# Sixteen last sums on GpSimd, eleven transposed copies on VectorE and a new order in an attention and highway kernel

## The chip, the cores and the metric

The kernel runs on one core of a Trainium2 chip. The metric is the device time of one execution in microseconds (us), median over runs. The engines are named as in the profile: PE (TensorE, matmuls), PEld (its weight loads), DVE (VectorE), ACT (ScalarE), POOL (GpSimd) and SP (SyncE, which here only issues DMAs).

## The reference

Sliding-window attention with four sink keys, then a highway layer. Batch 4, 8 heads, 768 positions, head size 64; the highway layer has 3072 tokens of 512.

```python
scores = scale * (q @ k.T)
keep = is_sink | ((rel >= 0) & (rel < 128))      # rel = query position - key position
a = exp(where(keep, scores, -1e9) - max);  a = a / (sum(a) + 1e-9)
x = (a @ v), heads side by side                  # (3072, 512)
H = maximum(x @ w_h, 0)
T = 1 / (1 + exp(-(x @ w_t + b_t)))
out = T * H + (1 - T) * x                        # float32
```

## The kernel before

The 3072 tokens are 24 tiles of 128; six tiles make a batch. A tile n goes through these steps, each a small function of the kernel:

- Loads: lq, lk, lv. Tiles 0 and 1 of q and k come in float32 through SP (q) and ACT (k), and DVE casts them (cvq, cvk). All others, v and the weights (lw_t, lw_h) are issued by POOL and cast on the way; each q or k tile of POOL goes into one of eight buffers. For batches 1 to 3, v comes in two halves (lv0, lv1).
- T (L258) transposes q and k on PE into PSUM, cT (L272) copies them to SBUF on ACT. pks (L278) puts a batch's four sink keys aside with small POOL copies, and issues the next batch's sink values.
- S0, S1 (L304) are the scores of four heads each, for this tile's keys and those of the tile before; E0, E1 (L320) their exponentials on ACT into float16; M0, M1 (L329) multiply them with a 0/1 mask on DVE, both inputs in SBUF. sk and es do the sink keys for two tiles.
- BA (L344) starts the tile's PSUM sum with the sink part, AV (L353) adds the weighted values and, in column 64 of each head, the sums of the weights. rec (L375) is their reciprocal on DVE, x (L380) the division on DVE out of PSUM, into xh.
- X (L387) transposes xh on PE, cX copies it to SBUF as xT: on ACT, or on DVE where the step is named cXd (L397).
- Tt (L407) and H (L422) multiply xT with the two weight matrices, four matmuls of 512 columns each. u (L417) is a tanh on ACT. On DVE: d (L430) is max(H, 0) - x, with H in PSUM; g (L436) turns the tanh into the sigmoid, SBUF to SBUF; ee (L442) is g * d, both in SBUF; od (L447) is the last sum xh + ee, both float16 in SBUF, into float32, and the SP queue stores it.

Constants: K1 to K5 (L210 to L244), pm and pb (L194 to L208, selects on POOL that make masks), lbt (L216, two loads of the bias on SP). K2 sets the bias rows, with two casts of one row of 512 on DVE (L227). A few matmuls on a zero tile (_FILL, L20) keep PE busy early.

The order is written out by hand: _STEPS (L21 to L55) is one list of steps, and each engine and each DMA queue takes its instructions in the order of that list. An instruction that waits holds up all that is behind it on its engine; a DMA issued by POOL stands in one line with POOL's computing. Buffers: four each for u, dd, gt and ee and for the output tile, seven each for xh and xT, one PSUM buffer for AV's and X's results.

Of the kernel before, what the change touches and what calls it, by code (L numbers as in the profile page):

```python
# [11 lines left out]
ALU = mybir.AluOpType  # L12
# [6 lines left out]

_FILL = {'T:0': 4, 'S1:0': 3, 'T:1': 1, 'S1:1': 3, 'S0:1': 2, 'S1:2': 1, 'T:3': 3}  # L20
_STEPS = """  # L21
    lk:0 lq:2 lsv:0 K4:0 pm:0 K1:0 cvk:0 lk:1 lbt:0 lq:0 cvq:0 T:0 cT:0 K3:0 S1:0 E1:0 S0:0 E0:0
    cvk:1 lq:1 cvq:1 T:1 K2:0 lq:3 lv:0 M1:0 cT:1 S1:1 E1:1 S0:1 M0:0 AV:0 lk:2 lk:3 rec:0 x:0 T:3
    E0:1 lv:1 T:2 M1:1 X:0 cT:2 cXd:0 M0:1 S0:2 AV:1 rec:1 x:1 cT:3 S1:3 lw_t:0 lk:4 pb:0 K5:0 pks:0
    E0:2 sv:6 E1:3 M1:3 M0:2 lq:4 S1:2 E1:2 sk:2 es:2 X:1 cX:1 Tt:0 u:0 T:4 cT:4 S0:3 lv:2 M1:2 E0:3
    lw_h:0 BA:2 AV:2 rec:2 x:2 M0:3 Tt:1 u:1 lq:5 g:1 lk:5 g:0 lv:3 X:2 cX:2 S1:4 H:0 d:0 E1:4 M1:4
    H:1 lq:7 T:5 S0:4 d:1 lk:7 ee:1 cT:5 E0:4 BA:3 AV:3 rec:3 lq:6 Tt:2 u:2 sk:4 es:4 x:3 od:1 X:3
    cX:3 S1:5 g:2 ee:0 M0:4 lv:4 E1:5 H:2 S0:5 d:2 E0:5 BA:4 AV:4 od:0 rec:4 lk:6 T:6 lv:5 ee:2 x:4
    cT:6 od:2 lv0:6 Tt:3 M0:5 u:3 X:4 lk:8 cX:4 T:7 cT:7 M1:5 S0:6 H:3 BA:5 AV:5 d:3 g:3 ee:3 lq:8
    E0:6 S1:6 E1:6 rec:5 S0:7 x:5 Tt:4 X:5 od:3 M1:6 E0:7 M0:7 u:4 g:4 T:8 S1:7 lv1:6 cX:5 E1:7 M0:6  # L30
    H:4 Tt:5 lk:9 d:4 lq:9 AV:6 M1:7 cT:8 u:5 ee:4 lk:10 S1:8 E1:8 rec:6 lq:10 x:6 pks:6 H:5 X:6
    od:4 d:5 S0:8 g:5 ee:5 T:9 cX:6 AV:7 rec:7 x:7 lk:11 Tt:6 E0:8 X:7 od:5 cT:9 S1:9 cXd:7 u:6 sk:8
    M0:8 lq:11 lk:13 g:6 E1:9 lk:12 es:8 lq:12 H:6 lq:13 T:10 cT:10 M1:8 d:6 ee:6 S0:9 E0:9 BA:8
    AV:8 rec:8 Tt:7 u:7 T:11 lk:14 cT:11 x:8 X:8 S1:10 od:6 cXd:8 H:7 M0:9 BA:9 E1:10 M1:9 S0:10 d:7
    AV:9 E0:10 rec:9 x:9 g:7 ee:7 M0:10 Tt:8 lq:14 u:8 T:12 X:9 od:7 g:8 cT:12 M1:10 lv0:12 cX:9
    sk:10 es:10 H:8 d:8 S1:11 E1:11 S0:11 E0:11 sv:12 BA:10 AV:10 rec:10 x:10 Tt:9 T:13 ee:8 u:9
    S0:12 E0:12 M1:11 X:10 lv1:12 M0:11 H:9 M0:12 S1:12 cX:10 BA:11 pks:12 lk:15 od:8 AV:11 rec:11
    cT:13 g:9 E1:12 T:14 cT:14 Tt:10 x:11 X:11 cX:11 d:9 ee:9 M1:12 S1:13 S0:13 H:10 od:9 u:10 g:10
    AV:12 rec:12 x:12 E0:13 Tt:11 lq:15 T:15 d:10 M0:13 E1:13 M1:13 lk:18 ee:10 u:11 g:11 X:12 S1:14
    H:11 d:11 cX:12 E1:14 cT:15 AV:13 od:10 S0:14 E0:14 Tt:12 sk:14 u:12 es:14 ee:11 S1:15 E1:15  # L40
    rec:13 lq:17 S0:15 x:13 X:13 od:11 lk:17 lk:16 M0:14 cX:13 M1:14 H:12 d:12 lq:20 T:17 g:12 BA:14
    AV:14 rec:14 x:14 E0:15 lq:16 T:16 M0:15 cT:17 lq:18 ee:12 Tt:13 X:14 lv0:18 M1:15 cT:16 H:13
    cX:14 S1:16 S0:16 u:13 d:13 od:12 E1:16 E0:16 lq:19 BA:15 lv1:18 g:13 AV:15 sk:16 rec:15 ee:13
    S0:17 es:16 E0:17 Tt:14 u:14 x:15 od:13 lk:19 lk:20 S1:17 M0:16 X:15 cX:15 E1:17 H:14 T:18 BA:16
    M1:16 M0:17 AV:16 d:14 Tt:15 cT:18 S0:18 T:19 pks:18 rec:16 g:14 u:15 x:16 X:16 cX:16 E0:18
    ee:14 od:14 H:15 M1:17 BA:17 M0:18 S1:18 g:15 lq:21 d:15 AV:17 rec:17 x:17 Tt:16 lk:21 cT:19
    S1:19 ee:15 E1:18 M1:18 T:20 X:17 cXd:17 u:16 g:16 H:16 od:15 AV:18 cT:20 E1:19 lq:22 rec:18
    x:18 S0:19 d:16 E0:19 M0:19 M1:19 Tt:17 u:17 S1:20 X:18 T:21 cX:18 H:17 cT:21 ee:16 lk:22 AV:19
    d:17 T:22 rec:19 E1:20 x:19 od:16 cT:22 g:17 sk:20 es:20 sv:18 S0:20 ee:17 M1:20 E0:20 M0:20
    X:19 Tt:18 u:18 lq:23 cX:19 od:17 H:18 d:18 S0:21 E0:21 S1:21 E1:21 BA:20 AV:20 rec:20 g:18  # L50
    lk:23 Tt:19 T:23 S1:22 u:19 x:20 M0:21 X:20 cX:20 ee:18 M1:21 cT:23 od:18 g:19 H:19 d:19 BA:21
    AV:21 E1:22 rec:21 S0:22 E0:22 Tt:20 ee:19 x:21 u:20 od:19 M0:22 M1:22 sk:22 S1:23 X:21 cX:21
    S0:23 H:20 es:22 BA:22 AV:22 g:20 d:20 rec:22 x:22 ee:20 E1:23 E0:23 M0:23 Tt:21 u:21 X:22 cX:22
    H:21 M1:23 BA:23 AV:23 d:21 g:21 rec:23 x:23 od:20 Tt:22 u:22 ee:21 g:22 od:21 X:23 cX:23 H:22
    d:22 ee:22 od:22 Tt:23 u:23 g:23 H:23 d:23 ee:23 od:23  # L55
"""


# [1 line left out]
def kernel(  # L60
# [13 lines left out]
    nc = tc.nc  # L74
    P = 128

    B, H, S, D = q.shape
# [44 lines left out]
    bt32 = const.tile([P, DM], FP32, tag="bt32")  # L122
    bt16 = const.tile([P, DM], FP16, tag="bt16")
# [70 lines left out]
    def pm():  # L194
        nc.gpsimd.affine_select(
            out=mask[:, 1, :], in_=mask[:, 1, :], compare_op=ALU.is_ge, fill=0.0,
            base=0, pattern=[[1, P]], channel_multiplier=-1)
        nc.gpsimd.affine_select(
            out=mask[:, 0, :], in_=mask[:, 0, :], compare_op=ALU.is_ge, fill=0.0,
            base=-1, pattern=[[-1, P]], channel_multiplier=1)  # L200

    def pb():
        nc.gpsimd.affine_select(
            out=bm, in_=bm, compare_op=ALU.is_ge, fill=0.0,
            base=0, pattern=[[-NSINK, H]], channel_multiplier=1)
        nc.gpsimd.affine_select(
            out=bm, in_=bm, compare_op=ALU.is_ge, fill=0.0,
            base=NSINK - 1, pattern=[[NSINK, H]], channel_multiplier=-1)  # L208

    def K1():  # L210
        nc.vector.tensor_copy(out=mask0, in_=mask[:, 1, :])
        nc.vector.memset(mask0[0:NSINK, :], 1.0)
        nc.vector.tensor_copy(out=mask1, in_=mask)
        nc.vector.memset(mask1[0:NSINK, 0, :], 1.0)

    def load_bt():  # L216
        nc.sync.dma_start(out=bt32[0:1], in_=moe_b_t.unsqueeze(0))
        nc.sync.dma_start(out=bt32[64:65], in_=moe_b_t.unsqueeze(0))

    def K2():  # L220
        nc.vector.memset(bt16, 0.0)
        nc.vector.memset(ones_row, 0.0)
        nc.vector.memset(ones1, 0.0)
        nc.vector.memset(ones1[0:1, :], 1.0)
        for r in (0, 64):
            nc.vector.memset(ones_row[r:r + 1, :], 1.0)
            nc.vector.tensor_copy(out=bt16[r:r + 1, :], in_=bt32[r:r + 1, :])  # L227

    def K3():
        for i in range(2):  # L230
            nc.vector.memset(ks_bd[i], 0.0)

    def K4():
        for vb in v_bat:
            nc.vector.memset(vb[:, 0:VBW].rearrange("p (m e) -> p m e", e=65)[:, :, D:D + 1], 1.0)
            nc.vector.memset(vb[:, VBW:VBW + 8], 0.0)
        for i in range(2):
            nc.vector.memset(vs_bd[i], 0.0)
            nc.vector.memset(es_t[i], 0.0)
# [10 lines left out]
    def warm_up(n):  # L250
        w = m_ps.tile([P, DM], FP32, tag="m", name="wps")
        for _ in range(n):
            nc.tensor.matmul(w, lhsT=warm[:, 0:P], rhs=warm, start=True, stop=True)

    qkT, tp_of, s_of, e_of, av_of, rec_of, g_of = {}, {}, {}, {}, {}, {}, {}
    xtp_of, xh_of, xT_of, t_of, u_of, h_of, dd_of, ee_of, sk_of = {}, {}, {}, {}, {}, {}, {}, {}, {}

# [116 lines left out]

    def rec(n):  # L375
        r = r_pool.tile([P, H], FP32, tag="rec", name="rec")
        nc.vector.reciprocal(out=r.unsqueeze(2), in_=av_of[n][:, :, 64:65])
        rec_of[n] = r

    def x(n):  # L380
# [63 lines left out]
        nc.vector.tensor_tensor(out=e, in0=g_of.pop(n), in1=dd_of.pop(n), op=ALU.mult)  # L444
        ee_of[n] = e

    def o(n):  # L447
        otok = o_pool.tile([P, DM], FP32, tag="otok", name="otok")
        nc.vector.tensor_tensor(out=otok, in0=xh_of.pop(n), in1=ee_of.pop(n), op=ALU.add)  # L449
        nc.sync.dma_start(out=out[n * P:(n + 1) * P, :], in_=otok)  # L450

    run = {
# [3 lines left out]
        "lsv": load_sink_v, "cvq": lambda n: convert("q", n), "cvk": lambda n: convert("k", n),  # L456
        "pm": lambda n: pm(), "pb": lambda n: pb(), "K1": lambda n: K1(), "K2": lambda n: K2(), "lbt": lambda n: load_bt(),
        "K3": lambda n: K3(), "K4": lambda n: K4(), "K5": lambda n: K5(),
        "T": T, "cT": cT, "pks": pks, "sv": lambda n: sink_v(n // NSC, nc.vector), "sk": sk, "es": es,
        "S0": lambda n: scores(n, 0), "S1": lambda n: scores(n, 1),  # L460
        "E0": lambda n: expo(n, 0), "E1": lambda n: expo(n, 1),
        "M0": lambda n: masked(n, 0), "M1": lambda n: masked(n, 1),
        "BA": BA, "AV": AV, "rec": rec, "x": x, "X": X, "cX": cX, "Tt": Tt, "u": u, "H": Hh,
        "cXd": lambda n: cX(n, nc.vector),
        "d": d, "g": g, "ee": ee, "od": o,
    }

    with tc.manual_schedule(engines={ENG.PE, ENG.DVE, ENG.Activation, ENG.SP, ENG.Pool}):
        first()
        for step in _STEPS.split():  # L470
            name, n = step.split(":")
# [36 lines left out]
```

## Time and profile before

| What | Value |
|---|---|
| Runs, us | 115.22, 115.41, 116.79 (median 115.41) |
| The profiled execution, us | 116.29 |
| Its span, first to last instruction, us | 114.6 |
| Mean granted PE clock over the span | 0.986 |
| Busy us: PE, DVE, ACT, POOL | 102.0, 102.2, 91.1, 60.8 |
| Instructions: PE, DVE, ACT, POOL | 1617, 236, 125, 79 |
| HBM read and written, MB | 21.01 and 6.29 |
| q and k loads through POOL | 44 of 128 KB, about 7 us from issue to landing |
| Chain that ended last, by engine | DVE 31%, DMA 24%, PE 19%, POOL 15%, ACT 5% |

In the profile a group is one line of the kernel on one engine: its name is output<-inputs, then the shapes, the count, the busy us of all and the mean ns of one, and the engine's idle time just before them with what ended it. POOL's busy time includes issuing its DMAs. A stretch of the timeline has its start, its length and its work; equal instructions behind one another are merged. The table of stretches has, for each, PE, PEld, DVE, ACT and POOL busy in us with the number of instructions, then the granted clock, the DMA share and GB/s. A row of waits has the engine and line, what it waited for, and us in total, times and the longest. The chain is followed back from the last instruction, at each step to what released it.

### The profile page before, as it was taken

How to read it: one execution, taken by the hardware profiler on the slowest of the kernel's cores; microseconds unless marked ns; L12 is line 12 of the kernel's file. 1: busy time of each engine (PE TensorE's matmuls, PEld its weight loads, DVE VectorE, ACT ScalarE, POOL GpSimd, SP SyncE). 2: the span in 40 equal slices, each digit the busy share in tenths (PEclk: the TensorE clock that was granted, in tenths of full speed). 3: DMA queues.
4: the chain of work that ended last, by engine and by line, in shares of the span. 5: the costliest groups of instructions: out<-in, count | busy, mean ns of one | idle time of the engine just before them, and what ended most of it. 6: DMA issues, size and time to landing. Idle time of an engine off the chain costs nothing.

```text
span 114.6 us, 3853 instructions
## 1 busy us (share of the span) xinstructions
PE 102.0 (89%) x1617; PEld 56.4 (49%) x1617; DVE 102.2 (89%) x236; ACT 91.1 (80%) x125; POOL 60.8 (53%) x79
## 2 busy tenths in 40 slices
PE   5956949999999899999999999999998999999910
PEld 2313535555555455556455655646554655644400
DVE  4649569699999999999999999999997999999990
ACT  3137699979999898989989999998898999982500
POOL 5999999796976199704999980003960000000000
PEclk9999999999999999999999999999999999999995
DMA  2999999999999999999999999991899222220332
GB/s 63 244 161 154 198 162 194 156 157 155 156 191 225 181 207 211 215 156 196 166 129 196 194 168 200 212 220 54 112 134 191 36 91 92 96 93 0 123 152 92
DMA packets 79540, 17.56 MB, mean 153 GB/s; under 512 B 75426, under 2 KB 76450, under 8 KB 79524
## 3 DMA queue, kind: packets, MB, share of 16 engines
q0 software_dynamic: 71904, 9.98, 132.0%
q1 hardware_dynamic: 5540, 6.82, 18.4%
q10 hardware_dynamic: 2080, 0.52, 2.0%
q8 instruction: 12, 0.20, 0.7%
q14 instruction: 4, 0.03, 0.1%
HBM read 21.01 MB, written 6.29 MB: 238 GB/s over the span
## 4 chain that ended last, share of the span: by engine, by line
DVE 31%; DMA 24%; PE 19%; POOL 15%; ACT 5%; issue 3%; POOLq 0%; ACTq 0%
DMA ksd<-in_k_dram 14%; DMA vb<-in_v_dram 10%; DVE e L335 8%; PE hps L426 6%; DVE otok L449 6%; DVE xh L382 5%; DVE dd L432 5%; POOL qsd L150 4%; PE av L368 3%; POOL ksd L150 3%; PE tps L414 3%; POOL v_all L146 3%; PE sps L316 3%; DVE gt L438 2%; DVE ee L444 2%
## 5 line engine op out<-in xcount | busy, mean ns | idle before, releaser
L324 ACT ACTIVATE e<-sps 128x1024 f16<-128x1024 f32 (+1 forms) x48 | 44.8, 961 | 2.2 <-PE sps L316 1.9
L274 ACT COPY qk<-tp 128x1024 f16<-128x1024 f16 x24 | 24.3, 1021 | 7.3 <-PE tp L268 7.3
L335 DVE TENSOR_TENSOR e<-e,mask 128x1024 f16<-128x1024 f16 (+1 forms) x48 | 29.2, 638 | 0.2
L426 PE MATMUL hps<-wh_sb,xT 128*128 128x512 f16 x96 | 24.7, 381 | 0.0
L414 PE MATMUL tps<-wt_sb,xT 128*128 128x512 f16 x96 | 24.7, 379 | 0.0
L150 POOL DMA_DIRECT2D ksd<-in_k_dram x22 | 19.9, 910 | 4.5 <-PE av L368 3.1
L150 POOL DMA_DIRECT2D qsd<-in_q_dram x22 | 20.1, 921 | 0.2
L419 ACT ACTIVATE u<-tps 128x512 f16<-128x512 f32 x24 | 14.5, 606 | 5.6 <-PE tps L414 5.4
L316 PE MATMUL sps<-qk 64*128 64x128 f16 x352 | 16.8, 217 | 1.7 <-ACT qk L274 1.7
L382 DVE TENSOR_TENSOR xh<-av,rec 128x512 f16<-128x512 f32 x24 | 16.5, 689 | 0.6
L432 DVE SCALAR_TENSOR_TENSOR dd<-hps,xh 128x512 f16<-128x512 f32 x24 | 16.4, 681 | 0.7 <-PE hps L426 0.7
L449 DVE TENSOR_TENSOR otok<-xh,ee 128x512 f32<-128x512 f16 x24 | 16.4, 683 | 0.1
L368 PEld LDWEIGHTS <-e 128*128 128x128 f16 x352 | 12.8, 97 | 5.5 <-DVE e L335 2.3
L316 PEld LDWEIGHTS <-qk 64*128 64x128 f16 x352 | 10.7, 94 | 8.6 <-issue 6.5
L404 ACT COPY xT<-xtp 128x512 f16<-128x512 f16 x20 | 11.8, 588 | 1.0 <-PE xtp L393 0.7
L368 PE MATMUL av<-vb,e 128*128 128x66 f16 x264 | 11.6, 194 | 0.6 <-DMA vb<-in_v_dram 0.4
L414 PEld LDWEIGHTS <-xT 128*128 128x128 f16 x96 | 8.2, 97 | 7.3
L426 PEld LDWEIGHTS <-xT 128*128 128x128 f16 x96 | 7.7, 98 | 8.0 <-issue 0.3
L285 POOL COPY ks<-qk 64x16 f16<-64x16 f16 x8 | 2.8, 349 | 16.2 <-ACT qk L274 16.0
L444 DVE TENSOR_TENSOR ee<-gt,dd 128x512 f16<-128x512 f16 x24 | 10.0, 417 | 0.3
L156 POOL DMA_DIRECT2D vb<-in_v_dram x6 | 8.7, 1449 | 1.2 <-DMA ksd<-in_k_dram 1.0
L438 DVE TENSOR_SCALAR gt<-u 128x512 f16<-128x512 f16 x24 | 8.6, 363 | 0.0
(66 smaller groups left out, 110.3 us busy)
## 6 DMA issues: line engine op xcount, KB each, us to landing
out_dram<-otok SPq DMA_DIRECT2D x24, 256.0 KB, 5.1
qsd<-in_q_dram POOLq DMA_DIRECT2D x22, 128.0 KB, 7.3
ksd<-in_k_dram POOLq DMA_DIRECT2D x22, 128.0 KB, 7.0
vb<-in_v_dram POOLq DMA_DIRECT2D x6, 384.0 KB, 10.8
v_all<-in_v_dram POOLq DMA_DIRECT2D x6, 128.0 KB, 7.0
kf<-in_k_dram ACTq DMA_DIRECT2D x2, 256.0 KB, 3.9
qf<-in_q_dram SPq DMA_DIRECT2D x2, 256.0 KB, 5.8
wt_sb<-in_moe_w_t_dram POOLq DMA_DIRECT2D x1, 512.0 KB, 6.9
```

The source lines that it names most:

```text
L150: nc.gpsimd.dma_start(out=sd, in_=dram(x, n))
L274: nc.scalar.copy(out=qk.rearrange("p j (a t) -> p a j t", a=2), in_=tp_of.pop(n)[:, :, 0:DM].rearrange("p a (j t) -> p a j t", t=64))
L316: nc.tensor.matmul(sps[:, hh, o:o + P], lhsT=kk[rows, hp, :], rhs=qT[rows, hp, :], start=True, stop=True)
L324: nc.scalar.activation(out=e.rearrange("p a b c d -> p a (b c d)"), in_=sps[:, :, 0:2 * np_ * P], func=AF.Exp, bias=_EXP_BIAS, scale=SCALE)
L335: nc.vector.tensor_tensor(out=ev, in0=ev, in1=m.unsqueeze(1).to_broadcast([P, 4, np_ * P]), op=ALU.mult)
L368: nc.tensor.matmul(av[:, g, 2 * hl + hh, 0:_AVN], lhsT=e[:, hh, hl, pc, :], rhs=v_cols(m, h), start=fresh, stop=False, skip_group_check=True)
L382: nc.vector.tensor_tensor(out=xh.rearrange("p (h d) -> p h d", d=D), in0=av_of.pop(n)[:, :, 0:D], in1=rec_of.pop(n).unsqueeze(2).to_broadc ...
L414: nc.tensor.matmul(t_of[n], lhsT=xT[:, kc, :], rhs=wt_sb[:, kc, :], start=False, stop=(kc == NOC - 1))
L419: nc.scalar.activation(out=uu, in_=t_of.pop(n), func=AF.Tanh, scale=0.5)
L426: nc.tensor.matmul(hps, lhsT=xT[:, kc, :], rhs=wh_sb[:, kc, :], start=(kc == 0), stop=(kc == NOC - 1))
L432: nc.vector.scalar_tensor_tensor(out=dd, in0=h_of.pop(n), scalar=0.0, in1=xh_of[n], op0=ALU.max, op1=ALU.subtract)
L449: nc.vector.tensor_tensor(out=otok, in0=xh_of.pop(n), in1=ee_of.pop(n), op=ALU.add)
```

## The change

It does five things.

- The last sum has two forms: `od:n` on DVE as before (tiles 0, 1, 2, 4, 6, 9, 15, 23) and `o:n` on POOL (the sixteen others). The POOL form gets a further dependency: it waits for the latest rec that stands ahead of it in the list.
- The copy of x's transpose is on DVE for tiles 0, 3, 4, 8, 10, 13, 14, 15, 16, 19 and 20 (before: 0, 7, 8, 17).
- The two casts of the bias go from K2 on DVE to a step K6 on ACT.
- The memsets of the sink tiles go from K4 to a step K7 that comes later.
- The list has another order throughout. _FILL is as before.

The code:

```diff
@@ -224,7 +224,10 @@
         nc.vector.memset(ones1[0:1, :], 1.0)
         for r in (0, 64):
             nc.vector.memset(ones_row[r:r + 1, :], 1.0)
-            nc.vector.tensor_copy(out=bt16[r:r + 1, :], in_=bt32[r:r + 1, :])
+
+    def K6():
+        for r in (0, 64):
+            nc.scalar.copy(out=bt16[r:r + 1, :], in_=bt32[r:r + 1, :])
 
     def K3():
         for i in range(2):
@@ -234,6 +237,8 @@
         for vb in v_bat:
             nc.vector.memset(vb[:, 0:VBW].rearrange("p (m e) -> p m e", e=65)[:, :, D:D + 1], 1.0)
             nc.vector.memset(vb[:, VBW:VBW + 8], 0.0)
+
+    def K7():
         for i in range(2):
             nc.vector.memset(vs_bd[i], 0.0)
             nc.vector.memset(es_t[i], 0.0)
@@ -252,6 +257,8 @@
         for _ in range(n):
             nc.tensor.matmul(w, lhsT=warm[:, 0:P], rhs=warm, start=True, stop=True)
 
+    last = {}
+    SYNC = mybir.DependencyInfo(mybir.DependencyClass.Sync, mybir.DependencyReason.DATA)
     qkT, tp_of, s_of, e_of, av_of, rec_of, g_of = {}, {}, {}, {}, {}, {}, {}
     xtp_of, xh_of, xT_of, t_of, u_of, h_of, dd_of, ee_of, sk_of = {}, {}, {}, {}, {}, {}, {}, {}, {}
 
@@ -374,7 +381,7 @@
 
     def rec(n):
         r = r_pool.tile([P, H], FP32, tag="rec", name="rec")
-        nc.vector.reciprocal(out=r.unsqueeze(2), in_=av_of[n][:, :, 64:65])
+        last["rec"] = nc.vector.reciprocal(out=r.unsqueeze(2), in_=av_of[n][:, :, 64:65])
         rec_of[n] = r
 
     def x(n):
@@ -444,9 +451,12 @@
         nc.vector.tensor_tensor(out=e, in0=g_of.pop(n), in1=dd_of.pop(n), op=ALU.mult)
         ee_of[n] = e
 
-    def o(n):
+    def o(n, eng):
         otok = o_pool.tile([P, DM], FP32, tag="otok", name="otok")
-        nc.vector.tensor_tensor(out=otok, in0=xh_of.pop(n), in1=ee_of.pop(n), op=ALU.add)
+        add = eng.tensor_tensor(out=otok, in0=xh_of.pop(n), in1=ee_of.pop(n), op=ALU.add)
+        if eng is nc.gpsimd:
+            tc.add_manual_dep(add.ins, last["rec"].ins.name, SYNC,
+                              reason="beside the PSUM reads that follow the reciprocal")
         nc.sync.dma_start(out=out[n * P:(n + 1) * P, :], in_=otok)
 
     run = {
@@ -456,13 +466,14 @@
         "lsv": load_sink_v, "cvq": lambda n: convert("q", n), "cvk": lambda n: convert("k", n),
         "pm": lambda n: pm(), "pb": lambda n: pb(), "K1": lambda n: K1(), "K2": lambda n: K2(), "lbt": lambda n: load_bt(),
         "K3": lambda n: K3(), "K4": lambda n: K4(), "K5": lambda n: K5(),
+        "K6": lambda n: K6(), "K7": lambda n: K7(),
         "T": T, "cT": cT, "pks": pks, "sv": lambda n: sink_v(n // NSC, nc.vector), "sk": sk, "es": es,
         "S0": lambda n: scores(n, 0), "S1": lambda n: scores(n, 1),
         "E0": lambda n: expo(n, 0), "E1": lambda n: expo(n, 1),
         "M0": lambda n: masked(n, 0), "M1": lambda n: masked(n, 1),
         "BA": BA, "AV": AV, "rec": rec, "x": x, "X": X, "cX": cX, "Tt": Tt, "u": u, "H": Hh,
         "cXd": lambda n: cX(n, nc.vector),
-        "d": d, "g": g, "ee": ee, "od": o,
+        "d": d, "g": g, "ee": ee, "o": lambda n: o(n, nc.gpsimd), "od": lambda n: o(n, nc.vector),
     }
 
     with tc.manual_schedule(engines={ENG.PE, ENG.DVE, ENG.Activation, ENG.SP, ENG.Pool}):
```

The new list:

```diff
+    lq:0 lk:0 lq:1 lk:1 lbt:0 lq:3 K4:0 K2:0 lk:2 cvq:0 cvk:0 lv:0 T:0 cT:0 lq:2 pm:0 S1:0 E1:0 K3:0
+    lv:1 lsv:0 cvq:1 lk:3 lw_t:0 pks:0 S0:0 lw_h:0 lk:4 E0:0 K1:0 lq:4 pb:0 cvk:1 K7:0 lv:2 T:1 M0:0
+    cT:1 lk:6 S1:1 E1:1 lk:5 S0:1 M1:0 AV:0 rec:0 x:0 T:2 X:0 cXd:0 E0:1 T:3 K6:0 M1:1 cT:2 S1:2
+    M0:1 cT:3 E1:2 K5:0 AV:1 rec:1 x:1 S1:3 Tt:0 sv:6 lq:5 E1:3 u:0 X:1 S0:2 cX:1 M1:3 E0:2 M1:2
+    lv:3 S0:3 lq:6 sk:2 es:2 lv0:6 lv:4 H:0 d:0 lk:7 BA:2 E0:3 T:4 cT:4 lq:7 M0:2 Tt:1 AV:2 u:1 S1:4
+    lv:5 H:1 M0:3 E1:4 g:0 ee:0 rec:2 x:2 od:0 X:2 cX:2 S0:4 E0:4 d:1 T:5 cT:5 g:1 BA:3 Tt:2 u:2
+    M1:4 ee:1 AV:3 S1:5 E1:5 H:2 lq:8 lk:8 M0:4 T:6 cT:6 rec:3 x:3 X:3 lv1:6 lq:9 g:2 d:2 S0:5 cXd:3
+    sk:4 es:4 lk:9 ee:2 od:1 E0:5 od:2 S0:6 BA:4 AV:4 rec:4 E0:6 Tt:3 pks:6 u:3 S1:6 x:4 T:7 M1:5
+    X:4 H:3 cT:7 E1:6 cXd:4 M0:5 BA:5 g:3 lq:10 d:3 ee:3 o:3 S0:7 E0:7 lk:10 AV:5 rec:5 x:5 Tt:4 T:8
+    u:4 g:4 lq:14 S1:7 M0:7 M1:6 M0:6 X:5 H:4 cX:5 d:4 Tt:5 ee:4 AV:6 rec:6 x:6 cT:8 S1:8 lq:11 E1:7
+    u:5 E1:8 H:5 od:4 M1:7 M1:8 X:6 cX:6 d:5 T:9 lk:11 S0:8 g:5 Tt:6 AV:7 cT:9 rec:7 x:7 E0:8 lk:12
+    u:6 S1:9 E1:9 g:6 M0:8 sk:8 es:8 M1:9 S0:9 X:7 cX:7 H:6 d:6 ee:6 E0:9 T:10 BA:8 lk:13 AV:8 cT:10
+    rec:8 x:8 od:6 lq:13 Tt:7 u:7 T:11 cT:11 lq:12 lv1:12 lk:14 X:8 cXd:8 S1:10 H:7 E1:10 BA:9
+    lv0:12 ee:5 S0:10 E0:10 M0:9 d:7 lq:15 AV:9 g:7 o:5 S1:11 rec:9 ee:7 sk:10 es:10 x:9 M0:10 o:7
+    Tt:8 lk:15 M1:10 S0:11 X:9 E1:11 u:8 g:8 H:8 lq:17 d:8 cX:9 T:12 BA:10 M1:11 E0:11 AV:10 cT:12
+    rec:10 Tt:9 u:9 x:10 T:13 S1:12 E1:12 M0:11 lq:18 X:10 cXd:10 cT:13 M1:12 lq:16 g:9 H:9 BA:11
+    ee:8 T:14 d:9 cT:14 o:8 AV:11 rec:11 x:11 Tt:10 ee:9 od:9 S1:13 u:10 g:10 S0:12 E0:12 X:11 cX:11
+    M0:12 pks:12 H:10 E1:13 d:10 lk:16 S0:13 E0:13 AV:12 rec:12 lk:17 x:12 sv:12 lv1:18 lk:18 Tt:11
+    u:11 M0:13 S1:14 lq:21 X:12 M1:13 cX:12 T:15 g:11 H:11 d:11 ee:11 o:11 AV:13 lk:20 rec:13 x:13
+    cT:15 ee:10 S0:14 lq:20 E1:14 E0:14 M0:14 Tt:12 S0:15 lq:19 u:12 X:13 sk:14 H:12 cXd:13 E0:15
+    T:16 M1:14 o:10 S1:15 sv:18 es:14 BA:14 cT:16 d:12 E1:15 AV:14 rec:14 x:14 Tt:13 u:13 lk:19
+    S0:16 E0:16 M1:15 T:17 X:14 cT:17 cXd:14 M0:15 H:13 BA:15 S1:16 AV:15 E1:16 d:13 sk:16 es:16
+    Tt:14 u:14 lv0:18 g:13 ee:13 o:13 g:12 S1:17 E1:17 rec:15 x:15 X:15 M0:16 cXd:15 M1:16 ee:12
+    g:14 T:18 H:14 BA:16 d:14 cT:18 o:12 S0:17 E0:17 AV:16 rec:16 x:16 Tt:15 u:15 lk:21 S0:18 S1:18
+    E0:18 X:16 M0:17 cXd:16 H:15 M1:17 E1:18 M1:18 T:19 cT:19 ee:14 BA:17 lk:22 T:20 cT:20 AV:17
+    d:15 Tt:16 u:16 S1:19 S0:19 o:14 rec:17 x:17 X:17 M0:18 H:16 pks:18 g:15 cX:17 lq:23 g:16 ee:15
+    od:15 AV:18 Tt:17 rec:18 x:18 d:16 X:18 E0:19 lq:22 M0:19 lk:23 E1:19 M1:19 u:17 ee:16 o:16
+    cX:18 S1:20 E1:20 g:17 T:21 H:17 d:17 AV:19 rec:19 cT:21 S0:20 Tt:18 E0:20 x:19 M1:20 S0:21 X:19
+    u:18 ee:17 o:17 E0:21 sk:20 M0:20 es:20 H:18 g:18 cXd:19 S1:21 E1:21 d:18 ee:18 T:22 cT:22 BA:20
+    AV:20 o:18 Tt:19 T:23 rec:20 x:20 u:19 M0:21 X:20 cXd:20 M1:21 S0:22 cT:23 H:19 E0:22 d:19 g:19
+    ee:19 BA:21 S1:22 E1:22 AV:21 rec:21 x:21 sk:22 Tt:20 S0:23 M0:22 es:22 u:20 M1:22 g:20 X:21
+    cX:21 H:20 d:20 o:19 ee:20 o:20 E0:23 S1:23 E1:23 BA:22 AV:22 rec:22 x:22 M1:23 Tt:21 u:21 M0:23
+    X:22 H:21 cX:22 BA:23 g:21 d:21 AV:23 rec:23 x:23 ee:21 o:21 H:22 d:22 X:23 cX:23 Tt:22 u:22
+    Tt:23 u:23 g:22 ee:22 o:22 H:23 d:23 g:23 ee:23 od:23
```

More of the change, by code (lines that the diff above doesn't have):

```diff
@@ L21 @@
 _STEPS = """
[L22 to L54, printed above, removed]
@@ L55 @@
-    d:22 ee:22 od:22 Tt:23 u:23 g:23 H:23 d:23 ee:23 od:23
+    lq:0 lk:0 lq:1 lk:1 lbt:0 lq:3 K4:0 K2:0 lk:2 cvq:0 cvk:0 lv:0 T:0 cT:0 lq:2 pm:0 S1:0 E1:0 K3:0
[3 more added lines that the diff above has]
+    lv:3 S0:3 lq:6 sk:2 es:2 lv0:6 lv:4 H:0 d:0 lk:7 BA:2 E0:3 T:4 cT:4 lq:7 M0:2 Tt:1 AV:2 u:1 S1:4
```

## Prediction

> **What bounds the kernel now.** I read the busy table by stage first, then the groups of instructions, then VectorE's waits, then the chain, and last two tiles that tell how GpSimd and VectorE get on. The stages (busy us of PE, weight loads, DVE, ACT, POOL, each with its count):
>
> ```profile
> 25.00:40.00 15.00, 14.19 (x232) 8.03 (x227) 14.67 (x33) 13.87 (x20) 9.65 (x13) 1.00 2.38 180
> 40.00:65.00 25.00, 24.44 (x438) 14.20 (x436) 24.61 (x52) 23.07 (x33) 19.41 (x23) 1.00 2.04 183
> 65.00:90.00 25.00, 24.43 (x432) 14.49 (x432) 23.88 (x53) 23.59 (x34) 8.85 (x12) 1.00 1.57 160
> 90.00:106.00 16.00, 15.70 (x226) 8.38 (x225) 15.92 (x36) 12.94 (x20) 0.00 (x0) 1.00 0.18 68
> 106.00:114.60 8.60, 3.36 (x21) 1.36 (x21) 5.35 (x11) 1.58 (x3) 0.00 (x0) 0.82 0.31 122
> ```
>
> From 25 to 106 us DVE is busy 14.67+24.61+23.88+15.92 = 79.1 of 81 us. ACT is at 73.5, so it has 7.5 us to spare. PE shows 78.8, but its matmuls overlap: the trace starts back-to-back 512-column matmuls 216 ns apart and shows each as 380 ns. With each matmul at the median start spacing of its kind, PE's 102 us shrink to some 80 over the whole span; the rest is waiting. DVE is the tightest, ACT next.
>
> The groups that the change touches, and those beside them:
>
> ```profile
> L335 DVE TENSOR_TENSOR e<-e,mask 128x1024 f16<-128x1024 f16 (+1 forms) x48 | 29.2, 638 | 0.2
> L382 DVE TENSOR_TENSOR xh<-av,rec 128x512 f16<-128x512 f32 x24 | 16.5, 689 | 0.6
> L432 DVE SCALAR_TENSOR_TENSOR dd<-hps,xh 128x512 f16<-128x512 f32 x24 | 16.4, 681 | 0.7 <-PE hps L426 0.7
> L449 DVE TENSOR_TENSOR otok<-xh,ee 128x512 f32<-128x512 f16 x24 | 16.4, 683 | 0.1
> L404 ACT COPY xT<-xtp 128x512 f16<-128x512 f16 x20 | 11.8, 588 | 1.0 <-PE xtp L393 0.7
> L402 DVE COPY xT<-xtp 128x512 f16<-128x512 f16 x4 | 1.7, 418 | 0.0
> L227 DVE CAST bt<-bt 1x512 f16<-1x512 f32 x2 | 1.2, 578 | 0.0
> ```
>
> A last sum (otok) is 683 ns on DVE, but the next instruction starts before it ends. The chain late in the span shows what one costs in time (start, us, what):
>
> ```profile
> 104.28 0.60 DVE dd L432
> 104.89 0.20 DVE gt L438
> 105.09 0.17 DVE rec L377
> 105.26 0.02 issue
> 105.29 0.69 DVE xh L382
> 105.98 0.60 DVE otok L449
> ```
>
> So 0.60 us each. From 88.6 us this chain is DVE alone. What DVE waited for (total, times, longest):
>
> ```profile
> DVE rec L377 <- PE av L368: 3.2, 5, 1.2
> DVE qh L168 <- DMA qf<-in_q_dram: 2.2, 2, 1.6
> ```
>
> Two tiles show GpSimd and VectorE in each other's way (duration min/median/max in ns), and two moments say when (a stretch is two copies):
>
> ```profile
> L285 POOL COPY ks<-qk x8: 191/288/752, 10.6 to 79.3; 64x16 f16<-64x16 f16 x8
> ```
> ```profile
> L438 DVE TENSOR_SCALAR gt<-u x24: 230/286/1229, 23.0 to 109.4; 128x512 f16<-128x512 f16 x24
> ```
> ```profile
> 53.20 1.11 POOL L285 COPY ks<-qk 64x16 f16<-64x16 f16 x2 [5.10 <-ACT qk L274]
> ```
> ```profile
> 79.08 0.45 POOL L285 COPY ks<-qk 64x16 f16<-64x16 f16 x2 [10.87 <-ACT qk L274]
> ```
>
> The same two GpSimd copies take 0.45 us beside an xh (which reads PSUM) and 1.11 beside a mask product (two SBUF inputs, 53.57 to 54.25; the second copy ends 0.06 after it). The other way round, a gt at 23.2 lasts 1229 ns while GpSimd issues a transfer (22.91 to 24.31), where it has 286 alone. So each makes the other wait, by what it reads.
>
> **The change, part by part.** (1) Sums. od stays for tiles 0, 1, 2, 4, 6, 9, 15 and 23. Up to xh of tile 23 (105.29 before), DVE did 20 sums and will do 7: 13 x 0.60 = 7.8 us off DVE's dense stretch. (2) Copies cXd rise from 4 to 11, all before that point: 7 x 0.36 (418 ns shown, 0.34 to the next start) = 2.5 us onto DVE; ACT gives up 7 x 0.588 = 4.1. Sum of (1) and (2): -5.3 on DVE.
>
> (3) The adds on GpSimd. No row shows one. Its selects take 193 ns at the least for 8 elements and about 300 for 128, so 0.9 ns per element: 0.65 us for 512 with one input, 1.1 if the second input is read after the first, 1.55 if the write counts too. I take 1.1, the one with two reads. 16 x 1.1 = 18 us on a POOL that is busy 61 of 115: hidden as POOL's time. The Trainium skill's page GPSIMD Engine Reference, section 3.1, has 4497 ns for 2048 elements, an estimate of 1.12 us for 512; the sum would be the same, and no run shows it yet.
>
> What an add costs DVE lies between 0 (it runs beside PSUM readers) and its whole 1.1 us (a two-input instruction stands still all the while). Which, I read from DVE's new order behind each ee. Behind tiles 8, 12, 14, 16 come rec, xh or dd for 1.3 us or more: 0. Behind 3, 11, 13, 18, 20 come rec and xh (0.82 us): about 0.35 each. Behind 7 and 19 xh alone: 0.5 each. Behind 5, 10, 17 a mask product starts first, GpSimd waits, then one PSUM reader covers part: 0.5, 0.7, 0.6. Together 4.6 us for the 14 adds before xh of tile 23. Ends: 0 and 14 x 1.1 = 15.4. I take 3.0, nearer to the listed sum than to either end, and below it because DVE, once relieved, waits for PE's av as it did for 3.2 us above, and an add in such a gap is free. The Trainium skill's page SBUF — State Buffer, section "Who interferes with whom", says that a VectorE instruction with two SBUF inputs and a GpSimd one that reads SBUF exclude each other, and that whichever starts first holds on for its whole length. The trace agrees for GpSimd's side (1.11 against 0.45); by that rule alone the sum would take 4.6 in place of 3.0.
>
> (4) The wait for the latest rec. In DVE's order ee:n stands behind that rec in 15 of the 16 cases, so the wait for ee, which was needed anyway, ends later: price 0. Only tile 19 is held, by rec of tile 21 just behind its ee: 0.2 us on an idle POOL. What queues behind a waiting add is q, k and v loads: lk:10, lk:15, lk:16, lk:20, lk:19, lk:21 and their fellows. Loads land about 7 us after issue; lk:21 was issued at 80.5 and T:21 waited for it (the chain's DMA piece of 6.81 us). In the new order it stands behind o:12, whose ee comes about xh of tile 16 (78.8 in the old time): no later. lk:15, issued at 54.8, moves to about 53 and T:15 needs it at 63. Price 0; if a load came late, its tile's T, cT and scores would slip by as much.
>
> (5) Start. q's first load goes ahead of two bias loads on SP's queue (issue 1.49, now about 0.81), the bias casts (1.2 us) go to ACT, part of K4's memsets go behind the first casts, pm's selects go behind two more loads on POOL (ready at 6 rather than 3.8; first used at 3.8, then about 9). M of tile 0 comes at about 11.2 instead of 11.9 at its end; against that, K6's casts stand before cT:2 on ACT, up to 2 x 0.59, where ACT had 0.56 idle; k of tile 3 is issued 1 us later. Between -1.2 and +0.6: I take -0.6. (6) End. Behind xh of tile 23 PE and ACT carry it (X, cX, Tt, H, 3.4 us), then dd, ee, otok and the store: three sums fewer save only what DVE delays PE, 0.3.
>
> Sum: -5.3 +3.0 -0.6 -0.3 = -3.2 us. The profiled execution is 116.29 (span 114.6 and 1.7 around it) and becomes 113.1; it lies 0.9 above the median of 115.41, which becomes **112.2**.
>
> **Rivals.** A, slower: the adds hold DVE for most of their length. With h us per add the change is -6.2 + 14h: zero at h = 0.44, over 2% slower at 0.61. At h = 0.75 it is +4.3: 119.7. For it: the 1.11 us above, the gt of 1229, and an add several times as long as those copies; against it: most adds have a PSUM reader behind their ee. The rule just named from the Trainium skill would be this rival if GpSimd always came first. B, no change: ACT and PE, at 73.5 and waiting on one another, don't follow a relieved DVE; only start and end remain plus a little, 114.5. For it: ACT is 91% busy; against: it loses 4.1 us itself, and where PE's weight loads wait for an engine, it is mostly DVE (xh and e). C: every add runs beside a PSUM reader, -6.2: 109.2. D: adds in POOL's queue make loads late; two tiles late by 2 us each give -3.2+4.0 = +0.8: 116.2, four 120.2. Against it: the places counted above. That the hold does nothing (15 of 16) is in my sum.
>
> **How the numbers follow.** Forecast (110.5 to 113.1: h from 0.1 to 0.3) 0.44, C 0.10, B 0.20, A 0.18, D 0.08. The range leaves out the lowest part of C and most of A: 109.0 to 118.0; the likeliest alone has 110.5 to 113.1. Under 113.1 is faster by over 2% (what a measurement of this kernel can tell from no change), over 117.7 slower: faster 0.44+0.10 = 0.54, same B and half of D = 0.24, slower A and half of D = 0.22.
>
> **What would show it.** Sixteen POOL sums of about 1.1 us; mask products, ee and gt stretched or started late beside them, by 0.2 us per sum on the mean; DVE busy some 5 us less and with idle gaps before rec; ACT 4 us less; first xh up to 1 us sooner. Wrong if an add takes 2 us or more, if gt or e stand still for whole adds (A), or if T waits for ksd at several tiles (D).

## The result and the profile after

The changed kernel takes 116.8 us (median of 20 runs, 116.58 to 117.11), the kernel before 116.72 in the runs beside it (20 runs, 115.22 to 118.9). The ratio is 1.007, 95% interval 1.0045 to 1.0094: no gain, and a small loss. Some executions of a kernel are some per cent longer at a lower granted clock, and every ratio here leaves them out, so it isn't the ratio of the two medians.

The stages of the changed kernel (PE, weight loads, DVE, ACT, POOL busy, each with its count):

```profile
25.00:40.00 15.00, 13.78 (x222) 7.99 (x222) 13.49 (x30) 12.43 (x18) 11.33 (x15) 1.00 2.38 186
40.00:65.00 25.00, 24.20 (x426) 13.95 (x425) 24.45 (x49) 22.56 (x32) 21.04 (x24) 1.00 2.11 184
65.00:90.00 25.00, 24.62 (x427) 14.78 (x426) 24.51 (x54) 22.69 (x31) 17.54 (x19) 1.00 1.60 154
90.00:106.00 16.00, 15.11 (x237) 8.40 (x235) 15.62 (x31) 11.90 (x17) 5.03 (x5) 1.00 0.26 87
```

DVE is as full as it was: 24.45 and 24.51 of 25 us, with sixteen sums gone. The groups say what fills it, first gt and ee of the kernel before, then the changed kernel's:

```profile
L438 DVE TENSOR_SCALAR gt<-u 128x512 f16<-128x512 f16 x24 | 8.6, 363 | 0.0
L444 DVE TENSOR_TENSOR ee<-gt,dd 128x512 f16<-128x512 f16 x24 | 10.0, 417 | 0.3
```
```profile
L342 DVE TENSOR_TENSOR e<-e,mask 128x1024 f16<-128x1024 f16 (+1 forms) x48 | 31.9, 685 | 0.0
L445 DVE TENSOR_SCALAR gt<-u 128x512 f16<-128x512 f16 x24 | 10.7, 447 | 1.6 <-ACT u L426 1.6
L451 DVE TENSOR_TENSOR ee<-gt,dd 128x512 f16<-128x512 f16 x24 | 10.5, 437 | 0.8
L456 POOL TENSOR_TENSOR otok<-xh,ee 128x512 f32<-128x512 f16 x16 | 19.4, 1215 | 25.9 <-DVE ee L451 18.3 <-DVE rec L384 4.3 <-issue 3.3
L456 DVE TENSOR_TENSOR otok<-xh,ee 128x512 f32<-128x512 f16 x8 | 5.4, 685 | 0.1
L409 DVE COPY xT<-xtp 128x512 f16<-128x512 f16 x11 | 4.6, 416 | 0.8 <-PE xtp L400 0.8
L439 DVE SCALAR_TENSOR_TENSOR dd<-hps,xh 128x512 f16<-128x512 f32 x24 | 16.3, 680 | 1.4 <-PE hps L433 1.4
L389 DVE TENSOR_TENSOR xh<-av,rec 128x512 f16<-128x512 f32 x24 | 16.6, 691 | 0.8
```

The mask products took 29.2 us and take 31.9, gt 8.6 and 10.7, ee 10.0 and 10.5: 5.3 us more for the same work. dd and xh, which read PSUM, are as they were. A GpSimd sum takes 1.15 us (up to 1.53 where it has to wait for VectorE). One that costs, tile 17's, on DVE and on POOL:

```profile
91.26 0.69 DVE L342 TENSOR_TENSOR e<-e,mask 128x1024 f16<-128x1024 f16 x1
91.86 1.25 DVE L445 TENSOR_SCALAR gt<-u 128x512 f16<-128x512 f16 x1
93.03 0.41 DVE L409 COPY xT<-xtp 128x512 f16<-128x512 f16 x1
```
```profile
91.43 1.53 POOL L456 TENSOR_TENSOR otok<-xh,ee 128x512 f32<-128x512 f16 x1 [1.37 <-DVE ee L451]
```

The sum is released at 91.43 behind a mask product that has begun; its 1.53 us are 0.38 more than a sum needs, so it gets through at about 91.8, as the mask product makes way. gt behind it, 0.29 us in the median, lasts 1.25 and ends just after the sum does (93.11 against 92.96). And one that is free, tile 16's:

```profile
88.89 0.68 DVE L439 SCALAR_TENSOR_TENSOR dd<-hps,xh 128x512 f16<-128x512 f32 x1
89.49 0.20 DVE L384 RECIPROCAL rec<-av 128x8 f32<-128x8 f32 x1
89.72 0.69 DVE L389 TENSOR_TENSOR xh<-av,rec 128x512 f16<-128x512 f32 x1
```
```profile
88.91 1.15 POOL L456 TENSOR_TENSOR otok<-xh,ee 128x512 f32<-128x512 f16 x1 [1.94 <-issue]
```

Three PSUM readers cover it, none is stretched.

Three points in time divide the span: the start of xh of tile 6, that of tile 23, and the end. Between the first two lie 17 tiles of steady work; I call this the steady stretch and read it from the trace of each kernel.

| Kernel | xh of tile 0 | xh of tile 6 | Steady stretch | Behind it |
|---|---|---|---|---|
| before | 13.3 | 39.7 | 65.6 | 9.3 |
| after | 12.2 | 39.7 | 66.0 | 9.3 |

Tile 0 comes 1.1 us sooner and tile 6 at the same time. In the steady stretch DVE has 12 sums fewer (-7.2 us from start to next start), 5 copies more (+1.7), mask products +3.0 (one more of them in it, 0.6), gt +2.3, ee and rec +0.7: it is back where it was.

### The profile page after: what moved, and what is told of

It reads as the page before. It is cut to its first block, busy times and chain, and to the rows that moved or that the text cites. A ratio compares the mean times of both kernels' runs of the same rounds, so it can differ in the third digit from the quotient of the medians.

```text
span 115.0 us, 3866 instructions
## 1 busy us (share of the span) xinstructions
PE 101.8 (89%) x1617; PEld 56.8 (49%) x1617; DVE 100.4 (87%) x225; ACT 89.4 (78%) x120; POOL 79.2 (69%) x95
## 4 chain that ended last, share of the span: by engine, by line
DVE 45%; DMA 18%; PE 16%; POOL 14%; issue 3%; DVEq 0%
DVE e L342 14%; DMA vb<-in_v_dram 11%; DVE xh L389 8%; DVE dd L439 7%; DMA wh_sb<-in_moe_w_h_dram 7%; DVE ee L451 5%; PE hps L433 5%; DVE gt L445 5%; POOL qsd L150 4%; PE tps L421 4%; POOL ksd L150 3%; POOL v_all L146 2%; PE av L375 2%; DVE otok L456 2%; DVE rec L384 2%
## 5 line engine op out<-in xcount | busy, mean ns | idle before, releaser
L456 POOL TENSOR_TENSOR otok<-xh,ee 128x512 f32<-128x512 f16 x16 | 19.4, 1215 | 25.9 <-DVE ee L451 18.3
L342 DVE TENSOR_TENSOR e<-e,mask 128x1024 f16<-128x1024 f16 (+1 forms) x48 | 31.9, 685 | 0.0
L426 ACT ACTIVATE u<-tps 128x512 f16<-128x512 f32 x24 | 14.5, 604 | 6.4 <-PE tps L421 6.2
L445 DVE TENSOR_SCALAR gt<-u 128x512 f16<-128x512 f16 x24 | 10.7, 447 | 1.6 <-ACT u L426 1.6
L451 DVE TENSOR_TENSOR ee<-gt,dd 128x512 f16<-128x512 f16 x24 | 10.5, 437 | 0.8
L411 ACT COPY xT<-xtp 128x512 f16<-128x512 f16 x13 | 7.6, 585 | 3.3 <-PE xtp L400 3.0
L400 PE MATMUL xtp<-ident,xh 64*128 64x64 f16 x192 | 6.9, 191 | 2.0 <-DVE xh L389 2.0
```

Of the source, the lines that this page charges most:

```text
L342: nc.vector.tensor_tensor(out=ev, in0=ev, in1=m.unsqueeze(1).to_broadcast([P, 4, np_ * P]), op=ALU.mult)
L445: nc.vector.tensor_scalar(out=gt, in0=u_of.pop(n), scalar1=0.5, scalar2=0.5, op0=ALU.mult, op1=ALU.add)
L456: add = eng.tensor_tensor(out=otok, in0=xh_of.pop(n), in1=ee_of.pop(n), op=ALU.add)
```

## The experiments

The theory behind the first four: while a GpSimd sum runs, VectorE's instructions whose inputs all lie in SBUF stand still (I call this the lock), and that is where the gain went. The rival: PE and ACT set the cadence, whatever VectorE has to do (coupling).

**e1: the sums cut short.** In place of the whole sum, on GpSimd (two fixed output tiles are cleared once, at the start):

```diff
+            otok = short[n % 2]
+            add = eng.tensor_tensor(out=otok[:, 0:8], in0=xh_of.pop(n)[:, 0:8], in1=ee_of.pop(n)[:, 0:8], op=ALU.add)
```

> The sixteen GpSimd sums are cut to 8 of 512 columns in two fixed tiles (504 columns of those sixteen output tiles are left out); place, waits and stores stay. Lock theory (what the sums freed on VectorE came back as mask products, gt and ee standing still while GpSimd adds): with adds of some 0.2 us the stretch goes, about 4 us of VectorE's time between tile 6 and tile 23, so about 113 us, and no mask product above 0.75 us. Rival, coupling theory (PE and ACT set the cadence whatever VectorE has to do): 116 to 117 us, VectorE with gaps instead.

Measured: 114.8 us, ratio 0.990 (0.986 to 0.994). Mask products are back at 29.5 us, steady stretch 63.7. The lock costs 2.0 us of the time, not 4: in the steady stretch DVE has 3.8 us less to do, of which 2.3 are gained and 1.5 became idle time (2.9 us idle against 1.4). The chain says who took over (its shares over the whole span, and a part of it):

```profile
PE 48%; DMA 18%; POOL 14%; DVE 13%; issue 3%; ACT 1%; DVEq 0%
```
```profile
48.36 0.97 PE hps L436 x4
49.33 0.22 PE tps L351
49.55 0.12 PE av L358
49.66 0.22 PE sps L326 x8
49.88 0.61 PE av L378 x16
50.49 0.33 PE sps L326 x8
50.82 0.55 PE sk L306 x8
51.38 0.86 PE tps L424 x4
```

For 16 us on end the chain doesn't leave PE; tile follows tile at 3.75 us (63.7/17).

**e2: write, don't read.** The sum becomes a memset of the same tile behind the same waits.

```diff
+            add = eng.memset(otok, 0.0)
+            tc.add_manual_dep(add.ins, eei[n].ins.name, SYNC, reason="after the product, as the sum")
```

> Each of the sixteen GpSimd sums becomes a memset of the same 128x512 float32 tile behind the same waits (the sum is left out in those sixteen tiles): GpSimd writes as much and reads nothing. If it is GpSimd's reading that holds VectorE's two-input instructions, mask products and ee are back at their 0.68 and 0.42 us, at least 2.5 us come back, about 114 us; gt may still be held. If writing holds them too, they stay stretched and the time stays at 116 to 117 us. Coupling theory: 116 to 117 us with no stretch.

Measured: 114.45 us, ratio 0.9895 (0.982 to 0.997). A memset is 0.52 us, and no mask product or ee is stretched:

```profile
L342 DVE TENSOR_TENSOR e<-e,mask 128x1024 f16<-128x1024 f16 (+1 forms) x48 | 29.5, 636 | 0.1
L458 POOL MEMSET otok<- 128x512 f32 x16 | 8.6, 540 | 33.5 <-DVE ee L451 17.9 <-issue 10.6 <-DVE rec L384 5.0
```

So it is GpSimd's reading that holds the instructions with two inputs in SBUF (the memset is also shorter, which this run doesn't separate).

**e3: all sums back on DVE, in the new order.**

```diff
-        "o": lambda n: o(n, nc.gpsimd), ...
+        "o": lambda n: o(n, nc.vector), ...
```

> New order and copies as they are, all 24 sums on VectorE. Lock theory: VectorE gets 12 x 0.60 = 7.2 us of sums between tile 6 and tile 23 and is rid of about 4 us of stretch, so about 3 us slower than the change, 119 to 120 us, gt and mask products unstretched. Coupling theory: VectorE has slack, at most 1 us slower, 117 to 118 us.

Measured: 120.75 us, ratio 1.043 (1.034 to 1.052), steady stretch 70.3; a little more than the lock theory had, far from the rival's 117 to 118. In this order the sixteen sums on GpSimd are worth 3.6% or some 4 us: the step works, the lock notwithstanding.

**e4: the copies back on ACT** (cXd for tiles 0 and 8 alone, cX for the nine others).

> Nine of the eleven copies of x's transpose go back to ACT (tiles 0 and 8 stay on VectorE); all else as in the change. If VectorE is the bound, 7 copies x 0.34 = 2.4 us come back between tile 6 and tile 23: about 114.5 us, ACT up by 9 x 0.55 = 5 us to about 94. If ACT sets the cadence as much as VectorE, 117 us or more (up to 119).

Measured: 118.35 us, ratio 1.0225 (1.017 to 1.028): the second case. DVE had 4.5 us idle in the steady stretch and ACT 93.5 us to do. Of the 1.5 us lost, 1.2 stand ahead of tile 6 (its xh comes at 41.0) and 0.6 in the steady stretch. In this order the copies on DVE are a gain.

Both theories held half, so the next three took work from the other side. e8, e9 and e10 leave out a quarter of x @ w_h:

```diff
-        for kc in range(NOC):
+        for kc in range(NOC - 1):
...
-                             start=(kc == 0), stop=(kc == NOC - 1))
+                             start=(kc == 0), stop=(kc == NOC - 2))
```

**e8: short sums and less PE.**

> The kernel of the short GpSimd sums (8 of 512 columns), and besides one of the four matmuls of each H is left out (a quarter of x @ w_h is missing): 17 x 0.216 = 3.7 us of PE between tile 6 and tile 23, nothing else touched. If PE is what takes over as soon as VectorE isn't held (the chain of the short sums ran on PE for most of 39 to 104 us), the time falls from 114.8 by 2 us or more, to 112.8 or less. Rival: a chain of latencies or ACT (23.3 of 25 us) holds the cadence: 114 to 115.

Measured: 112.7 us, ratio 0.978 (0.969 to 0.9875), steady stretch 62.1; the chain is back on DVE (41%, PE 19%).

**e9: the changed kernel with less PE.**

> The changed kernel with whole sums on GpSimd, one of four matmuls of each H left out (a quarter of x @ w_h is missing). If VectorE, held by the adds, is the bound of the changed kernel, at most 0.7 us is won: 116 or more. If PE is a bound beside it, it falls by 1.5 us or more, below 115.3.

Measured: 114.77 us, ratio 0.993 (0.989 to 0.997), steady stretch 64.05: 2 us less than the change. PE bounds beside DVE.

**e10: the kernel before with less PE.**

> The kernel before, one of four matmuls of each H left out (a quarter of x @ w_h is missing). VectorE was busy 98% there: if it alone bounds, at most 0.7 us is won against the runs of before beside it (ratio 0.994 or more). If PE bounds too, ratio 0.985 or less.

Measured: ratio 0.989 (0.981 to 0.997), steady stretch 64.1 against 65.6. The ratio lies between the two cases and its interval holds both; the steady stretch, read in one trace of each, speaks for the second: PE was a bound before the change.

**e7: without batch 1's value loads.**

```diff
+        if b == 1:
+            if part == 0:
+                nc.gpsimd.memset(v_bat[0], 1.0)
+            return
```

> The changed kernel without the two loads of batch 1's values (384 KB each; a memset stands in, so tiles 6 to 11 are computed with ones as values). Tile 6's division stood at 39.7 us in both kernels, whatever came before. Load theory (the stream of loads pins tile 6, and so the shorter start was lost): tile 6's division comes at 38.7 us or sooner and about 1 to 2 us of the time goes, 115 to 116. Rival (compute pins it): tile 6 within 0.4 us of 39.7, 116.5 or more.

Measured: 114.83 us, ratio 0.994 (0.990 to 0.998), so 2 us less than the change; tile 6's xh at 39.0. The time is that of the load theory, but tile 6 came only 0.8 us sooner and not 1.0; the rest is in the steady stretch (65.1). The stream of loads eats a part of the shorter start; that it does so at tile 6 alone is not shown.

**e5: no hold.**

```diff
-            tc.add_manual_dep(add.ins, last["rec"].ins.name, SYNC,
-                              reason="beside the PSUM reads that follow the reciprocal")
```

> The changed kernel, its GpSimd sums waiting for ee alone. By the list, the hold ends a wait later only for tile 19. Expected: same as the change within 0.4 us (116.4 to 117.2). If the hold matters at all places, at least 1 us away.

Measured: 116.64 us, ratio 1.0075 (1.004 to 1.011), the change's own. The hold does nothing.

**e6: the old order with the sums on GpSimd** (od becomes o for the sixteen tiles, at the same places in the list, with the hold).

> Only the sixteen sums moved to GpSimd with the hold; order, copies and start as in the kernel before. Read from the old order: adds stand VectorE still by some 8.5 us in all between tile 6 and tile 23 against 7.2 us of sums freed. Lock theory: no gain or a little loss, ratio 1.00 to 1.015 to the kernel before. If the lock's price doesn't depend on the order, as in the change (4.1 us): ratio below 0.99. If it is the new order that costs, this is clearly faster than the change.

Measured: 136.28 us, ratio 1.177 (1.164 to 1.190). No theory had that. It is POOL's queue: the sums hold up the loads behind them, and PE waits for loads that it found ready before. In e6:

```profile
PE av L370 <- DMA vb<-in_v_dram: 5.5, 2, 4.4
PE tp L270 <- DMA ksd<-in_k_dram: 5.2, 3, 2.7
PE tp L270 <- DMA qsd<-in_q_dram: 3.8, 3, 1.6
```

That is 14.5 us, where such waits come to 1.0 us in the kernel before and 1.0 in the changed kernel. DVE isn't what holds it, with 19 us idle in a steady stretch of 80.5. e11 shows the queue at work with half the sums.

**e11: the old order, eight sums on GpSimd, no hold.**

> Order, copies and start of the kernel before; only eight sums (tiles 3, 4, 5, 6, 11, 13, 16, 19), behind whose ee a rec, xh or dd comes next, go to GpSimd, without the hold. VectorE: 8 x 0.60 freed, about 8 x 0.3 held, 2.4 us net. At the half price that the runs with less PE work show: about 1 us faster than before, ratio 0.985 to 0.995. If VectorE were the only bound: 0.98 or less. If GpSimd's queue delays loads: 1.0 or more.

Measured: 130.32 us, ratio 1.115 (1.103 to 1.127): the last case, many times over. POOL in the kernel before, and in e11, at the same loads:

```profile
25.18 0.90 POOL L150 DMA_DIRECT2D qsd<-in_q_dram  x1
27.12 1.41 POOL L156 DMA_DIRECT2D vb<-in_v_dram  x1 [1.05 <-DMA ksd<-in_k_dram]
```
```profile
26.03 0.90 POOL L150 DMA_DIRECT2D qsd<-in_q_dram  x1
34.95 1.16 POOL L451 TENSOR_TENSOR otok<-xh,ee 128x512 f32<-128x512 f16 x1 [8.03 <-DVE rec L379]
36.06 1.45 POOL L156 DMA_DIRECT2D vb<-in_v_dram  x1
```

The sum stands in POOL's line ahead of the second half of batch 1's values and waits 8.03 us for DVE; the load goes out at 36.06 in place of 27.12, and tile 6's xh comes at 43.7 in place of 39.7. So it goes on: the second half of batch 2's values goes out at 57.0 in place of 46.7, that of batch 3's at 81.5 in place of 64.9.

**e12: the changed order mended** (AV of tile 7 ahead of Tt of tile 6; ee of tiles 5, 7 and 17 moved to stand ahead of PSUM readers).

> The changed kernel with AV of tile 7 ahead of Tt of tile 6, and ee of tiles 5, 7 and 17 moved to where PSUM readers follow: some 1.3 us less standing still for VectorE, and 1 us that the new order lost between tiles 6 and 7. At half price each about 1 us: 115.3 to 116.2. If only VectorE counts: 114.5. If neither: 116.8.

Measured: 116.19 us, ratio 1.0015 (0.997 to 1.006), just inside the 115.3 to 116.2 of the half price: 0.6 us less than the change, steady stretch 64.8. It draws level with the kernel before and doesn't beat it; no kernel here that computes everything beat the kernel before.

**e13: thirteen sums cut short in the kernel before.** It prices a us of DVE by itself.

```diff
+        if n in (3, 5, 7, 8, 10, 11, 12, 13, 14, 16, 17, 18, 19):
+            otok = short[n % 2]
+            nc.vector.tensor_tensor(out=otok[:, 0:8], in0=xh_of.pop(n)[:, 0:8], in1=ee_of.pop(n)[:, 0:8], op=ALU.add)
```

> The kernel before with thirteen last sums (tiles 3, 5, 7, 8, 10 to 14, 16 to 19) cut on VectorE to 8 of 512 columns in two fixed tiles (504 columns of those thirteen output tiles are left out); nothing moves, no GpSimd sum, no other order. It prices the prediction's step of 13 x 0.60 us: some 13 x 0.5 = 6.5 us of VectorE less. If VectorE alone bounds: ratio 0.95 or less. Joint bound (PE and VectorE together, half price or less): ratio 0.97 to 0.985. If PE alone: 0.99 or more.

Measured: ratio 0.994 (0.990 to 0.9975): the third case. In its trace xh of tile 0 comes at 16.0 us in place of 13.3 (mean granted clock 0.86 in the first 25 us, and two memsets of 0.49 us more, which clear its two fixed output tiles). The stages below have a clock of 1.00, so the steady stretch can be read: 64.4 us, 1.2 less than before. Its stages:

```profile
40.00:65.00 25.00, 24.71 (x442) 14.47 (x442) 23.55 (x54) 23.52 (x33) 17.15 (x20) 1.00 2.08 177
65.00:90.00 25.00, 24.82 (x428) 14.59 (x422) 22.16 (x54) 23.97 (x35) 10.36 (x13) 1.00 1.70 169
```

DVE falls to 22.16 of 25 us, PE stays at 24.82, and in the steady stretch rec waits 3.0 us for PE's av where it waited 0.2. Twelve of the thirteen sums lie in that stretch: some 6 us less for DVE bring 1.2 us there, and the thirteen bring 0.6% of the time.

**e14: the new order alone** (all sums on DVE as in e3, copies on DVE for tiles 0, 7, 8 and 17).

> The new order, but all 24 sums on VectorE and the copies of x's transpose on VectorE for tiles 0, 7, 8 and 17 as before: what is left is the order with its new start. If the order costs nothing: ratio to the kernel before 0.995 to 1.01. If the order, made for other engine loads and for a GpSimd queue with adds in it, costs by itself: 1.015 or more. If its start alone counted: 0.99.

Measured: 123.7 us, ratio 1.065 (1.060 to 1.070), steady stretch 71.7. In one row: 1.065 with the new order alone, 1.043 with the copies on DVE too, 1.007 with the sums on GpSimd too.

## Why the prediction was wrong

The time, 116.8, lies in the wide range but not where it was forecast: -3.2 us was predicted and the ratio is 1.007. In the number rival D (116.2) came nearest, and that is luck: its late loads aren't there, as PE waits for loads 1.0 us in all in both kernels. In the mechanism rival B came nearest (no change, 114.5: PE and ACT don't follow a relieved VectorE), though VectorE wasn't relieved either. By the steps:

- **What bounds (the first part): wrong, and the step that failed.** The prediction took PE for slack, since its matmuls at the median start spacing came to 80 us and "the rest is waiting". The median leaves out what each change from one kind of matmul to the next takes: four matmuls of H hold the chain for 0.97 us, not 4 x 0.216 = 0.86. In e1's steady stretch of 63.7 us all matmuls at the median spacing of their kind come to 51.4. Its 151 changes, nine a tile, take 8.2 more, waits before them included, and 4.1 are due to kinds that start in pairs (scores 3 to 16 ns apart, then 40 to 53), whose median says little. (Over the whole span of the kernel before I get 75 us from the spacings within a kind and 89 with those to the next kind, so the 80 doesn't come out again.) With the lock gone (e1), PE has 48% of the chain, DVE 13%, and the steady stretch is 63.7 us; the kernel before stood at 65.6, only 1.9 us above that pace. So step (1) priced 13 x 0.60 = 7.8 us one for one where, in the kernel before, some 6 us are worth 1.2 (e13). Less PE work in the kernel before, 17 x 0.216 = 3.7 us in the steady stretch, brings 1.5 there (e10): both bound it.
- **The sums and the lock (3): right.** 1.15 us a sum, 1.1 forecast. The durations above the usual beside the fourteen sums ahead of tile 23's xh add up to 3.5 us (tile 17 has 0.96, 7 has 0.58, 19 has 0.45, 5 and 11 some 0.37; 3, 8, 10, 12, 14 and 16 nothing), read as 4.6 and taken as 3.0. On the time it is 2.0 us (e1). The Trainium skill's page GPSIMD Engine Reference, section 3.1, has the figure from which 1.12 us was estimated for the sum; the trace agrees, with 1.15. The Trainium skill's page SBUF — State Buffer, section "Who interferes with whom", says that an instruction with two SBUF inputs contends with a GpSimd one that reads SBUF and not with one that only writes; e2 agrees, with mask products at 636 ns on the mean against 685.
- **The copies (2): wrong sign.** I put them at +2.5 us on DVE with ACT's relief worth nothing. In the new order they are worth -2% (e14 to e3), and taking them back costs 1.5 us (e4). That speaks for ACT, busy 91% of 25 to 106 us before, not being a spare engine; which wait carries it isn't shown.
- **The order: costed at nothing but its start.** It costs 6.5% by itself (e14). What it does with this is make room in POOL's queue: the same sums in the old order cost 17.7% (e6). Rival D had the mechanism and the counting held for the new order (no load late by it); what failed to be seen is that this order is the price of it. On DVE it has a price too, which the prediction put at nothing. In the steady stretch the forecast's terms come to -7.2 for twelve sums, +1.7 for five copies and +3.0 for the lock, so -2.5; DVE's work came out 0.6 us up. GpSimd's sums cost 3.8 (the change against e3), but gt, ee and rec take 1.8 more in the new order even where no sum is on GpSimd (e3, with a gt of 1.31 us beside a transfer that POOL issues), and one mask product more (0.6) falls into the stretch. Which of the order's moves cost most is not settled; e12 found 0.6 us in four of them.
- **The hold (4): right.** e5 is the change again. That no load of the new order comes late by it was right too (1.0 us of PE's waits, as before).
- **Start (5) and end (6): sized wrongly.** Tile 0 came 1.1 us sooner, against about 0.7 in the working, and nothing was left of it at tile 6; the forecast kept 0.6. Behind tile 23's xh it is 9.3 us in both kernels; 0.3 was forecast.
- **The likeliest range.** By the prediction's own formula, h from 0.1 to 0.3 gives 110.6 to 113.4, not 110.5 to 113.1.

In the order in which they were put on, the parts are +6.5% for the new order, -2.2 for the copies, -3.6 for the sums; each is the price beside what is already there. The sums' gain is there, and the order that they need takes it. What the copies and the sums would bring in an order that costs nothing isn't shown.

## What to carry to other kernels

Before a microsecond off the fullest engine is priced at a microsecond, take it off in a run that does nothing else (a shorter instruction in the same place), and do the same to the next engine; with three engines at 91 to 98%, the price here was a fifth (e13) to some six tenths (e1). A compute instruction on a queue that also issues loads holds every load behind it until its own operands are there, so look at what stands behind it before looking at what it costs. Work moved to GpSimd was free here beside VectorE instructions that read PSUM, and held those with both inputs in SBUF, and gt twice; read the order of VectorE's instructions behind the releasing one to see which it meets.

## What the runs showed of the hardware

- A GpSimd sum that has to wait for VectorE got in at the end of the instruction that was running, even though the next one stood ready: the sum of tile 17 ended 1.53 us after its release, 0.38 more than an unhindered one takes, and gt behind it, whose input was ready at 91.13, lasted 1.25 us instead of 0.29.
- gt (one input in SBUF, float16) is held by transfers that GpSimd issues: in e2, where GpSimd reads no sum, one took 1.31 us, starting 0.26 us into the issue of a value load that took 1.45. GpSimd's memsets there didn't hold it: four gt beside one took 0.285 to 0.289 us.
- In e11 the granted clock fell twice, each time behind a stretch in which PE was short of work; it was 0.957 on the mean. The slices of PE and of the clock:

```profile
PE   6847689999990699698999953699999899999930
PEclk9999999999999689999999999559999999999998
```

PE's empty slices (0 and 6, then 5, 3 and 6) stand a slice or two ahead of the clock's 6 and 8, and 5 and 5. Single slices of 4 and 6 elsewhere have no drop behind them, so it isn't a rule. If the one brings the other, late loads cost twice; no run here separates the two.
